# Linear attention with norm and a gated convolution FFN: g_norm as rows, batch 0 by one cast queue, spread products in pairs, a new order, unread products

## Chip, cores and metric

The kernel runs on one core of a Trainium2 chip, in one launch. The metric is the device time in microseconds; the kernel before takes 195.0, the median of three runs (194.63 to 196.04).

## The reference

Eight batches, eight heads, 576 positions, head size 64; the FFN goes from 512 to 1024 and back. All inputs and the output are float32.

```python
kv = np.einsum('bhsd,bhse->bhde', k, v)
out = np.einsum('bhsd,bhde->bhse', q, kv)
rms = np.sqrt(np.mean(out * out, axis=-1, keepdims=True) + 1e-06)
x = out / rms * g_norm            # then (batch, seq, heads * 64) = (8, 576, 512)
h = np.maximum(x @ w_in, 0.0)     # (8, 576, 1024)
conv_out = sum(conv_w[k] * hp[:, k:k + S, :] for k in range(3))   # hp: h padded by one row of zeros on each side
gate = 1.0 / (1.0 + np.exp(-conv_out))
return (h * gate) @ w_out         # (8, 576, 512)
```

## The kernel before

Everything is kept with channels on the partitions and positions on the free axis. The work is cut into small operations with names, and one long string, ORDER, lists them by hand: a loop at the end of the kernel takes the tokens in turn and calls the function of that name. Each engine then runs its own instructions strictly in that order (the last loop of the kernel ties each instruction to the one before it on its engine). A token such as `hm.0.2@2` calls `hm(0, 2)` and gives it buffer slot 2 of its ring. So a buffer's slot, and with it what an operation has to wait for, is written in the order too. There are three PSUM slots of two banks each, ring "a" (heads' transposes, attention output, hidden products, spread products), and two of one bank, ring "b" (kv products, sums of squares, output rows).

For batch b and head pair t (0 to 3) the operations are these.

- `Lq`, `Lk`, `Lv` load one batch of q, k, v from POOL's queue and cast them to bfloat16 on the way (L276). `Li` and `Lo` load halves of w_in and w_out the same way. Batch 0 is loaded in `pre`: head pairs 0 and 1 in float32 by SyncE's queue into a staging tile (L206), cast by `ca` on VectorE (k, v) and ScalarE (q, L305); pairs 2 and 3 by POOL's queue (L217).
- `kv` (L319) makes the 64 by 64 products of k and v of a head; `kvc` copies them into a block diagonal tile, on VectorE for batch 0 and on ScalarE for the others. `qt` transposes q for two head pairs (`qt0` for one, batch 0; L343), and `qc` copies the result on VectorE (`qc0` on ScalarE). `ot` (L373, L374) multiplies the two.
- `sq` squares and `oc` copies that output on ScalarE. `ss` (L427) adds up the squares of all four head pairs into 32 rows each, four products with 32 columns of output. `ln` takes the reciprocal root, and `sl` splits it on VectorE into bfloat16 parts. `sp` (L454) spreads these over the 64 channels of each head: two products per head pair, with all 128 rows of the parts and a selecting matrix, `spread`, of 2048 columns. `mu` (L460) multiplies output, g_norm and root on VectorE. Batch 0 goes another way: `on` spreads and adds in one product, `nl` takes the root, `mu0` multiplies.
- `hm` (L471) is the product with w_in for one block f of 128 hidden channels, eight products of 288 columns; `re` (L479) is the relu on ScalarE. `ta` (L493, L494) multiplies by two of the three taps, `aa` (L500) and `ab` (L506) add, `sg` (L512) is the sigmoid on ScalarE, `mg` (L518) the gating product. A convolution index c stands for one batch or two, by CONV.
- `om` (L528) is the product with w_out for a block m of 128 rows of a pair p of batches, eight products of 512 columns, in two halves for pairs 0 and 3; `ea` (L534) copies it on ScalarE and `st` (L539) stores it by SyncE's queue.
- `ct` and `pc` bring conv_w into channel layout and scale it; `pl`, `ps`, `pn` make the constants sel, spread, na and nb on VectorE. g_norm is loaded straight onto the partitions, as 128 elements of 4 bytes (L209).

The order puts batch 0 through attention first, then batches 1 to 7 in parts between the hidden products.

## Time and profile before

| | us |
|---|---|
| median of three runs (lowest, highest) | 195.0 (194.63, 196.04) |
| span of the profiled execution (the page gives no other time of it) | 192.5 |
| TensorE busy in it | 171.1 (89%) |
| ScalarE busy | 153.5 (80%) |
| VectorE busy | 148.8 (77%) |
| first product of TensorE | 10.31 |
| first product with w_in | 25.90 |
| last product's end, by the chain | 188.75 |

The span runs from the first to the last instruction. The shares are means over the whole span; the stretches differ. A product's record holds its latency, so the start of the next product tells better than the length what one costs. "Granted clock" is what the throttle gave TensorE.

### The profile page before, as it was taken

How to read it: one execution, taken by the hardware profiler on the slowest of the kernel's cores; microseconds unless marked ns; L12 is line 12 of the kernel's file. 1: busy time of each engine (PE TensorE's matmuls, PEld its weight loads, DVE VectorE, ACT ScalarE, POOL GpSimd, SP SyncE). 2: the span in 40 equal slices, each digit the busy share in tenths (PEclk: the TensorE clock that was granted, in tenths of full speed). 3: DMA queues.
4: the chain of work that ended last, by engine and by line, in shares of the span. 5: the costliest groups of instructions: out<-in, count | busy, mean ns of one | idle time of the engine just before them, and what ended most of it. 6: DMA issues, size and time to landing. Idle time of an engine off the chain costs nothing.

```text
span 192.5 us, 4249 instructions
## 1 busy us (share of the span) xinstructions
PE 171.1 (89%) x1753; PEld 106.9 (56%) x1753; DVE 148.8 (77%) x279; ACT 153.5 (80%) x246; POOL 25.7 (13%) x39
## 2 busy tenths in 40 slices
...
DMA  4999999999999997999950000441040010170874
GB/s 135 207 236 204 203 204 203 204 204 206 186 203 204 182 130 118 137 120 188 208 185 5 0 3 0 165 167 54 0 163 3 0 54 3 54 272 0 327 266 170
DMA packets 26517, 26.84 MB, mean 139 GB/s; under 512 B 1388, under 2 KB 21892, under 8 KB 26500
## 3 DMA queue, kind: packets, MB, share of 16 engines
...
q10 hardware_dynamic: 196, 0.01, 0.1%
q14 instruction: 4, 0.03, 0.1%
...
## 4 chain that ended last, share of the span: by engine, by line
PE 70%; DVE 11%; ACT 8%; DMA 6%; issue 2%; SPq 1%; ACTq 0%
PE h_ps L471 28%; PE om_ps L528 27%; DMA stg<-in_q_dram 6%; PE qt_ps L343 4%; PE sp_ps L454 4%; PE kv_ps L319 3%; ACT sq L388 2%; PE o_ps L374 2%; DVE taps L493 2%; DVE taps L500 2%; DVE taps L506 2%; DVE taps L494 1%; ACT o L393 1%; ACT h L479 1%; DVE h L518 1%
## 5 line engine op out<-in xcount | busy, mean ns | idle before, releaser
L471 PE MATMUL h_ps<-xT,w_in_sb 128*128 128x288 bf16 x512 | 70.1, 290 | 0.7 <-ACT o L393 0.3
L528 PE MATMUL om_ps<-w_out_sb,h 128*128 128x512 bf16 x288 | 66.7, 379 | 0.1
L471 PEld LDWEIGHTS <-w_in_sb 128*128 128x128 bf16 x512 | 50.0, 99 | 17.1 <-issue 1.5
L479 ACT ACTIVATE h<-h_ps 128x576 bf16<-128x576 f32 x64 | 40.6, 658 | 9.3 <-PE h_ps L471 9.0
L528 PEld LDWEIGHTS <-h 128*128 128x128 bf16 x288 | 27.8, 98 | 30.2 <-issue 0.7
L512 ACT ACTIVATE taps<-taps,cw 128x576 bf16<-128x576 bf16 (+1 forms) x48 | 42.9, 933 | 1.0 <-DVE taps L506 0.9
L534 ACT ACTIVATE row<-om_ps 128x512 f32<-128x512 f32 x36 | 21.8, 605 | 10.7 <-PE om_ps L528 10.4
L518 DVE TENSOR_TENSOR h<-h,taps 128x1152 bf16<-128x1152 bf16 (+1 forms) x24 | 22.7, 953 | 5.7 <-ACT taps L512 5.7
L500 DVE TENSOR_TENSOR taps<-taps 128x1152 bf16<-128x1152 bf16 (+1 forms) x24 | 23.0, 958 | 0.5
L343 PE MATMUL qt_ps<-ident,q_sb 96*64 96x96 bf16 x384 | 12.6, 221 | 12.0 <-ACT q_sb L305 11.9
L506 DVE TENSOR_TENSOR taps<-taps,h 128x1152 bf16<-128x1152 bf16 (+1 forms) x24 | 22.9, 956 | 0.5
L493 DVE TENSOR_SCALAR taps<-h,cw 128x576 bf16<-128x576 bf16 (+1 forms) x48 | 20.8, 434 | 2.5 <-ACT h L479 2.5
L460 DVE SCALAR_TENSOR_TENSOR xT<-o,g_sb,sp_ps 128x576 bf16<-128x576 f32 x28 | 21.2, 810 | 1.8 <-PE sp_ps L454 1.8
L494 DVE TENSOR_SCALAR taps<-h,cw 128x576 bf16<-128x576 bf16 (+1 forms) x48 | 20.3, 423 | 0.0
L343 PEld LDWEIGHTS <-q_sb 96*64 96x64 bf16 x384 | 10.4, 120 | 15.9 <-ACT q_sb L305 12.4
L388 ACT ACTIVATE sq<-o_ps 128x576 bf16<-128x576 f32 x28 | 18.1, 673 | 0.1
L393 ACT ACTIVATE o<-o_ps 128x576 f32<-128x576 f32 x28 | 17.8, 662 | 0.0
L374 PE MATMUL o_ps<-qT,kvbd 128*128 128x512 bf16 x32 | 12.7, 409 | 0.0
...
L368 DVE COPY qT<-qt_ps 128x1152 bf16<-128x1152 bf16 x14 | 10.4, 754 | 1.7 <-PE qt_ps L343 1.4
L454 PE MATMUL sp_ps<-wparts,spread 128*128 128x288 bf16 x56 | 9.9, 287 | 1.0 <-ACT h L479 0.7
L276 POOL DMA_DIRECT2D q_sb<-in_q_dram x8 | 6.0, 748 | 34.5 <-PE qt_ps L343 29.0
...
## 6 DMA issues: line engine op xcount, KB each, us to landing
...
```

The costliest lines, as they stand in the source:

```text
L343: nc.tensor.transpose(ps[i * D:(i + 1) * D, r * PS:(r + 1) * PS], qkv["q", b][:, 2 * t + i, r * D:(r + 1) * D], ident[:PS, :PS])
L388: nc.scalar.activation(by_r(s), natural(o), AX.Square)
L471: nc.tensor.matmul(ps[:, e, :HS], w_in_sb[:, t, f * P:(f + 1) * P], x[:, t, e * HS:(e + 1) * HS], start=(t == 0), stop=(t == NT - 1))
L479: nc.scalar.activation(T["h", b // 2][:, f, b % 2, :].rearrange("p (e n) -> p e n", e=2), T["hm", b, f][:, :, :HS], AX.Relu)
L493: nc.vector.tensor_scalar_mul(tap[:, 0, f % 2, :n, 8:8 + S], h[:, f], cw[:, f:f + 1])
L494: nc.vector.tensor_scalar_mul(tap[:, 1, f % 2, :n, :S], h[:, f], cw[:, 2 * NF + f:2 * NF + f + 1])
L500: nc.vector.tensor_add(tap[:, 1, :, :n, :S], tap[:, 0, :, :n, 7:7 + S], tap[:, 1, :, :n, 1:1 + S])
L506: nc.vector.tensor_add(y, y, h[:, 2 * j:2 * j + 2])
L512: nc.scalar.activation(y, y, AX.Sigmoid, scale=cw[:, NF + f:NF + f + 1])
L518: nc.vector.tensor_mul(h, h, T["tap", c, j][:, 1, :, :n, :S])
L528: nc.tensor.matmul(T["om", p, m], h[:, f, m * P:(m + 1) * P], w_out_sb[:, f, :], start=(f == 0), stop=(f == NF - 1))
L534: nc.scalar.activation(T["os", p, m], T["om", p, m], AX.Copy)
```

## The change

Six things change.

- g_norm is loaded as a 25th row of the tile that holds conv_w, in two pieces of 64 elements, and comes onto the partitions by the same transpose (`ct`, `pg`). The scaled taps get a tile of their own, cwn.
- Of batch 0 only k and v of head pair 0 go by SyncE's queue and the staging tile. All else goes by POOL's cast queue in the order q0, k1, v1, q1, k2, ..., and the identity's select comes behind the first two of these loads.
- `sp` makes two head pairs at once. Each product takes the 32 rows of the parts that belong to its head pair, at that row of the array (tile_position), and the two head pairs' products alternate. It takes two slots of ring "a". `spread` has 512 columns instead of 2048.
- The tokens may choose the engine: a colon and 1 moves a relu, `oc`, `ea` or `kvc` to VectorE and a q copy to ScalarE. In the new order 7 relus, 9 `oc`, 5 `ea` and 7 `kvc` are on VectorE (the kvc of batch 0 were there before), and 3 of 4 `qc0` and 4 of 14 `qc` on ScalarE. An `oc` on VectorE waits for ScalarE's `sq` of the same output. `pl` moves to POOL.
- `unread` issues n products of 512 columns on a tile of ones, into a PSUM slot that nobody reads: 11, 9, 2, 2, 3 and 6, all ahead of hm.0.0.
- The order is a new one. Batches 4 and 5 are loaded and their kv made before the first product with w_out, and w_out is loaded behind batch 5. `al` allocates the tiles of x and h, whose slots the tokens now give.

```diff
@@ ORDER @@
-pre@0,0,0,1 ca.q.0 qt0.0@0 qc0.0@0 ca.k.0 ca.v.0 kv.0.0.1@0 kvc.0.0.1.0 kvc.0.0.1.1 ot.0.0@1 sq.0.0@0 on.0@2
...
+pre@0,0,0 ca.k.0 ps pi ca.v.0 unread.11@0 kv.0.0.1@0 ct@1 Lv.1.0@1 qt0.0.0@0 Lq.1.0@1 Lk.1.0@1 pg kv.0.1.1@1
+unread.9@1 qt0.0.2@1 Li.0 Lq.1.2 qt0.0.1@2 pc kvc.0.0.1.0@0 qc0.0.0:1@0 kvc.0.1.1.0:1 kvc.0.0.1.1:1 al.x0@0
+qc0.0.2:1@1 al.h1@0 kvc.0.1.1.1 al.h0@1 ot.0.0@0 al.x1@1 sq.0.0@0 unread.2@1 on.0.0@1 nl.0.0@0 kv.0.2.1@0 qc0.0.1:1
+kvc.0.2.1.0 kvc.0.2.1.1 unread.2@1 ot.0.2@1 sq.0.2@1 unread.3@2 on.0.2@2 mu0.0.0 ot.0.1@0 nl.0.2@1 qt0.0.3@2 Lv.1.2
+mu0.0.2 sq.0.1@2 qc0.0.3 Lk.1.2 kv.0.3.1@1 kvc.0.3.1.1 on.0.1@1 nl.0.1@2 qt.1.0@2 kvc.0.3.1.0:1 mu0.0.1 ot.0.3@1
+sq.0.3@3 kv.1.0.2@0 on.0.3@0 qc.1.0@2 nl.0.3@3 mu0.0.3 kvc.1.0.2.0:1@1 Li.1 unread.6@2 hm.0.0@2 hm.0.2@0 kvc.1.0.2.1
+hm.0.3@1 re.0.0:1 pl re.0.2 ot.1.1@2 ta.0.0@0 re.0.3:1 qt.1.1@0 sq.1.1@4 hm.0.1@1 pn Lk.2.0@0 Lv.2.0@0 kv.1.2.2@1
+re.0.1 kvc.1.2.2.0 ot.1.0@1 kvc.1.2.2.1 sq.1.0@5 oc.1.0@4 qc.1.1@3 ta.0.2@1 ta.0.1 oc.1.1:1@5 ot.1.3@0 sq.1.3@6
...
+ta.1.1 oc.3.0@7 qt.4.0@0 re.1.4 sl.1@0 aa.1.0 re.1.2 Lq.5.0@1 sp.3.0@2,1 mu.3.0 mu.3.1 qc.4.0:1@4 Lv.5.0@1 Lk.5.0@1
+sp.2.1@0,2 mu.2.2 mu.2.3 Lo.0 kv.4.0.4@0 Lo.1 sg.0.4 kvc.4.0.4.0@0 kvc.4.0.4.1 sp.2.0@1,0 mu.2.1 mu.2.0 sg.0.5
+ot.4.1@2 sq.4.1@0 qt.5.0@0 oc.4.1@7 ot.4.2@1 sq.4.2@1 mg.0.2 hm.2.2@2 qc.5.0@0 ta.1.2@0 oc.4.2@6 ot.4.3@0 re.2.2
+qt.5.1@1 ab.1.0 sq.4.3@2 oc.4.3@0 hm.1.5@2 qc.5.1@1 sg.1.1 sp.3.1@0,1 kv.5.0.4@1 re.1.5 kvc.5.0.4.0@1 ta.1.3 al.x2@0
+mu.3.3 mu.3.2 hm.2.0@2 kvc.5.0.4.1 sg.1.0 hm.3.2@1 re.2.0 re.3.2 Lv.7.0@0 ot.5.1@0 ot.5.3@2 sq.5.3@3 aa.1.1 mg.1.0
+ab.1.1 om.0.3.0@0 ot.4.0@1 om.0.1.0@1 sg.1.2 sg.1.3 oc.5.3:1@1 Lq.7.0@0 ta.1.4@1 ta.1.5 sq.5.1@4 ot.5.0@2 om.0.3.4
+sq.4.0@5 oc.5.1:1@3 sq.5.0@6 om.0.1.4 hm.3.3@0 ea.0.3:1@0 oc.5.0@2 oc.4.0@4 aa.1.2 mg.1.1 re.3.3 ss.4@0 ot.5.2@2
+sq.5.2@7 hm.3.0@1 ss.5 hm.3.1@0 ln.2@0 re.3.1 ta.1.6@0 Lk.7.0@0 oc.5.2:1@5 ab.1.2 hm.2.4@2 re.3.0 ta.1.7 qt.7.1@0
...
+st.0.0 st.0.1 st.0.5 ta.3.7 sg.2.6 ss.7 mg.2.3 hm.5.4@1 ea.0.7@2 st.0.2 re.5.4 hm.5.0@2 hm.4.0@0 ln.3@0 aa.3.3
+om.1.4.0@0 sl.3@0 ea.1.4@1 ab.3.3 re.5.0 hm.4.1@1 om.1.8.0@1 re.4.1 re.4.0 sp.6.0@2,1 mu.6.1 om.1.5.0@0 sp.7.1@0,1
+st.0.6 ea.1.8@3 om.1.1.0@1 ta.3.0@0 mu.7.3 hm.4.4@1 mu.6.0 mu.7.2 hm.4.3@2 sg.3.6 sg.3.7 hm.5.1@0 mg.3.3 ea.1.1@4
...
+st.1.5 sg.5.1 sg.5.0 ea.3.1@4 aa.5.2 ab.5.2 mg.5.0 st.3.0 re.7.6:1 ta.5.6@0 ta.5.7 sg.5.4 ea.3.3@5 om.2.2.0@0 sg.5.5
+aa.5.3 om.2.5.0@1 st.2.0 ab.5.3 ea.2.2@3 om.3.7.0@0 mg.5.2 ea.2.5@6 st.2.2 sg.5.6 st.3.3 sg.5.7 st.2.6 om.2.1.0@1
+st.2.5 mg.5.3 ea.2.1@7 om.3.7.4 ea.3.7@1 om.3.5.0@1 om.3.8.0@0 om.3.5.4 ea.3.5@3 om.3.8.4 ea.3.8@5 om.3.6.0@1
+om.3.4.0@0 om.3.6.4 st.3.7 st.2.1 st.3.5 om.3.4.4 ea.3.6:1@2 st.3.8 st.3.2 st.3.1 st.3.6 ea.3.4@6 st.3.4
...
+    NC = 3 * NF
+    cw_rows = consts.tile([NC + 1, P], FP32, name="cw_rows")
+    cw = consts.tile([P, NC + 1], FP32, name="cw")
+    g_sb = cw[:, NC:NC + 1]
+    cwn = consts.tile([P, 3, NF], FP32, name="cwn")
+    fill = consts.tile([P, 512], BF16, name="fill")
...
-    spread = consts.tile([P, NT * 4, 2, D], BF16, name="spread")
-    bg = consts.tile([P, NT, 8], BF16, name="bg")
+    spread = consts.tile([P, 4, 2, D], BF16, name="spread")
+    bg = consts.tile([P, 8], BF16, name="bg")
...
@@ -200,74 +205,81 @@
     def pre():
         for x in "qkv":
             qkv[x, 0] = ring(x, [PS, H, R * D], BF16, name=x + "_sb")
-        T["stg"] = ring("h", [PS, 3, 2, 2, R * D], FP32, name="stg")
-        for t in range(2):
-            for x in "kvq":
-                nc.sync.dma_start(out=T["stg"][:, "kvq".index(x), t], in_=heads(x, 0, 2 * t, 2))
-        nc.scalar.dma_start(out=cw_rows, in_=moe_conv_w.rearrange("k (f p) -> (k f) p", p=P))
+        T["stg"] = work.tile([PS, 2, 2, R * D], FP32, name="stg", tag="h0", bufs=1)
+        for i, x in enumerate("kv"):
+            nc.sync.dma_start(out=T["stg"][:, i], in_=heads(x, 0, 0, 2))
+        nc.scalar.dma_start(out=cw_rows[:NC], in_=moe_conv_w.rearrange("k (f p) -> (k f) p", p=P))
         for i in range(2):
-            nc.scalar.dma_start(out=g_sb[i * D:(i + 1) * D, :], in_=g_norm.unsqueeze(1))
+            nc.scalar.dma_start(out=cw_rows[NC:, i * D:(i + 1) * D], in_=g_norm.unsqueeze(0))
+        nc.vector.memset(fill, 1.0)
         nc.vector.memset(ident, 0.0)
-        nc.gpsimd.affine_select(
-            out=ident, in_=ident, compare_op=AL.not_equal, fill=1.0,
-            base=0, pattern=[[-1, P]], channel_multiplier=1)
-        for t in range(2, NT):
-            for x in "kvq":
-                nc.gpsimd.dma_start(out=qkv[x, 0][:, 2 * t:2 * t + 2, :], in_=heads(x, 0, 2 * t, 2))
         nc.vector.memset(kvbd[0], 0.0)
...
-        nc.vector.tensor_copy(ident32, ident[:3 * NF, :3 * NF])
+        for n, (x, t) in enumerate([(x, t) for t in range(NT) for x in "kvq" if t or x == "q"]):
+            if n == 2:
+                nc.gpsimd.affine_select(
+                    out=ident, in_=ident, compare_op=AL.not_equal, fill=1.0,
+                    base=0, pattern=[[-1, P]], channel_multiplier=1)
+            nc.gpsimd.dma_start(out=qkv[x, 0][:, 2 * t:2 * t + 2, :], in_=heads(x, 0, 2 * t, 2))
+
+    @op
+    def pi():
+        nc.vector.tensor_copy(ident32, ident[:NC + 1, :NC + 1])
         for t in taps:
             nc.vector.memset(t[:, 0, :, :, 7:8], 0.0)
             nc.vector.memset(t[:, 1, :, :, S:S + 1], 0.0)
 
     @op
     def ct():
-        T["cw"] = ring("b", [P, 3 * NF], FP32, name="cw_ps", padded_shape=[P, 512])
+        T["cw"] = ring("b", [P, NC + 1], FP32, name="cw_ps", padded_shape=[P, 512])
         nc.tensor.transpose(T["cw"], cw_rows, ident32)
 
     @op
+    def pg():
+        nc.vector.tensor_copy(cw, T["cw"])
+
...
     @op
     def pl():
-        nc.vector.memset(sel, 0.0)
+        nc.gpsimd.memset(sel, 0.0)
         for c in range(4):
             for i in range(2):
                 at = c * 2 + i
-                nc.vector.memset(
+                nc.gpsimd.memset(
                     sel[i * D:(i + 1) * D, c, :].rearrange("p (g c) -> p g c", c=8)[:, :3, at:at + 1], 1.0)
     @op
     def ps():
-        nc.vector.tensor_add(bg, idv[:, :, 0, :], idv[:, :, 1, :])
-        nc.vector.tensor_add(bg, bg, idv[:, :, 2, :])
+        nc.vector.tensor_reduce(
+            bg, ident.rearrange("p (t g c) -> p c t g", t=NT, g=4)[:, :, :, :3],
+            axis=mybir.AxisListType.XY, op=AL.max)
         nc.vector.tensor_copy(
-            spread.rearrange("p a i d -> p (a i) d"),
-            bg.rearrange("p t c -> p (t c)").unsqueeze(2).to_broadcast([P, NT * 8, D]))
+            spread.rearrange("p a i d -> p (a i) d"), bg.unsqueeze(2).to_broadcast([P, 8, D]))
...
     @op
     def ca(x, t):
-        to, fr = qkv[x, 0][:, 2 * t:2 * t + 2, :], T["stg"][:, "kvq".index(x), t]
-        if x == "q":
+        nc.vector.tensor_copy(qkv[x, 0][:, 2 * t:2 * t + 2, :], T["stg"][:, "kv".index(x)])
+
+    def last():
+        return nc.cur_bb.bb.instructions[-1]
+
+    def after(ins, other):
+        if ins.engine != other.engine:
+            tc.add_manual_dep(
+                ins, other.name,
+                mybir.DependencyInfo(mybir.DependencyClass.Sync, mybir.DependencyReason.DATA), reason="bank")
+
+    def copy(to, fr, on_act):
+        if on_act:
             nc.scalar.activation(to, fr, AX.Copy)
         else:
             nc.vector.tensor_copy(to, fr)
@@ -325,11 +348,9 @@
     @op
     def kvc(b, t0, n, i):
         half = slice(i * D, (i + 1) * D)
-        to, fr = kvbd[b % 2][half, t0:t0 + n, half], T["kvps", b, t0][half]
-        if b == 0:
-            nc.vector.tensor_copy(to, fr)
-        else:
-            nc.scalar.activation(to, fr, AX.Copy)
+        if slots:
+            T["kvbd", b] = kvbd[slots.pop(0)]
+        copy(T["kvbd", b][half, t0:t0 + n, half], T["kvps", b, t0][half], pick[0] == 0)
 
...
-    @op
-    def qc0(t):
+    def qt0(b, t):
+        T["qt0", b, t] = ring("a", [P, 1024], BF16, name="qt_ps", padded_shape=[P, 2048])
+        transposes(T["qt0", b, t], b, t)
+
+    @op
+    def qc0(b, t):
         if t % 2 == 0:
-            T["q0", t // 2] = ring("qT", [P, 2, S], BF16, name="qT")
-        T["qT", 0, t] = T["q0", t // 2][:, t % 2, :]
-        nc.scalar.activation(by_r(T["qT", 0, t]), natural(T["qt0", t][:, :S]), AX.Copy)
+            T["q0", b, t // 2] = ring("qT", [P, 2, S], BF16, name="qT")
+        T["qT", b, t] = T["q0", b, t // 2][:, t % 2, :]
+        copy(by_r(T["qT", b, t]), natural(T["qt0", b, t][:, :S]), pick[0] == 1)
...
-        nc.vector.tensor_copy(s, T["qtps", b, u][:, :, :S])
+        copy(s, T["qtps", b, u][:, :, :S], pick[0] == 1)
+
+    @op
+    def unread(n):
+        nfill[0] = n
+        fills(ring("a", [P, 1024], FP32, name="unread_ps"))
+
+    def fills(ps):
+        for _ in range(nfill[0]):
+            nc.tensor.matmul(ps[:, :512], fill[:, :P], fill, start=True, stop=True)
...
     @op
     def ot(b, t):
         ps = T["ot", b, t] = ring("a", [P, 1024], FP32, name="o_ps")
-        mm576(ps, kvbd[b % 2][:, t, :], T["qT", b, t])
+        fills(ps)
+        mm576(ps, T["kvbd", b][:, t, :], T["qT", b, t])
...
+        T["sqi", b, t] = last()
 
     @op
     def oc(b, t):
         s = T["o32", b, t] = ring("o32", [P, S], FP32, name="o32")
-        nc.scalar.activation(by_r(s), natural(T["ot", b, t][:, :S]), AX.Copy)
-
+        copy(by_r(s), natural(T["ot", b, t][:, :S]), pick[0] == 0)
+        after(last(), T["sqi", b, t])
+
+    @op
+    def on(b, t):
+        ps = T["on", b, t] = ring("a", [P, 1024], FP32, name="on_ps")
+        fills(ps)
+        mm576(ps, ones, T["sq", b, t])
+
...
+    @op
+    def al(what):
+        p = int(what[1:])
+        if what[0] == "x":
+            T["x", p] = ring("xT", [P, NT, 2, S], BF16, name="xT")
+        else:
+            T["h", p] = ring("h", [P, NF, 2, S], BF16, name="h")
 
     def x_tile(b):
-        if ("x", b // 2) not in T:
-            T["x", b // 2] = ring("xT", [P, NT, 2, S], BF16, name="xT")
         return T["x", b // 2][:, :, b % 2, :]
...
     @op
-    def sp(b, t):
+    def sp(b, u):
         g = NG[b]
         bi = NORM[g].index(b)
-        ps = T["sp", b, t] = ring("a", [P, 2, 512], FP32, name="sp_ps")
+        for t in (2 * u, 2 * u + 1):
+            T["sp", b, t] = ring("a", [P, 2, 512], FP32, name="sp_ps")
         for e in range(2):
-            nc.tensor.matmul(
-                ps[:, e, :HS], spread[:, t * 4 + 2 * bi + e, :, :].rearrange("p i d -> p (i d)"), T["w", g],
-                start=True, stop=True)
+            for t in (2 * u, 2 * u + 1):
+                rows = slice(t * 32, (t + 1) * 32)
+                nc.tensor.matmul(
+                    T["sp", b, t][:, e, :HS], spread[rows, 2 * bi + e, :, :].rearrange("p i d -> p (i d)"),
+                    T["w", g][rows], start=True, stop=True, tile_position=(t * 32, 0))
...
     @op
     def hm(b, f):
         ps = T["hm", b, f] = ring("a", [P, 2, 512], FP32, name="h_ps")
         x = x_tile(b)
+        fills(ps.rearrange("p e n -> p (e n)"))
...
     @op
     def re(b, f):
-        if b % 2 == 0 and f == 0:
-            T["h", b // 2] = ring("h", [P, NF, 2, S], BF16, name="h")
-        nc.scalar.activation(
-            T["h", b // 2][:, f, b % 2, :].rearrange("p (e n) -> p e n", e=2),
-            T["hm", b, f][:, :, :HS], AX.Relu)
+        to = T["h", b // 2][:, f, b % 2, :].rearrange("p (e n) -> p e n", e=2)
+        fr = T["hm", b, f][:, :, :HS]
+        if pick[0] == 0:
+            nc.scalar.activation(to, fr, AX.Relu)
+        else:
+            nc.vector.tensor_scalar(to, fr, 0.0, None, op0=AL.max)
...
-        nc.vector.tensor_scalar_mul(tap[:, 0, f % 2, :n, 8:8 + S], h[:, f], cw[:, f:f + 1])
-        nc.vector.tensor_scalar_mul(tap[:, 1, f % 2, :n, :S], h[:, f], cw[:, 2 * NF + f:2 * NF + f + 1])
+        nc.vector.tensor_scalar_mul(tap[:, 0, f % 2, :n, 8:8 + S], h[:, f], cwn[:, 0, f:f + 1])
+        nc.vector.tensor_scalar_mul(tap[:, 1, f % 2, :n, :S], h[:, f], cwn[:, 2, f:f + 1])
...
-        nc.scalar.activation(T["os", p, m], T["om", p, m], AX.Copy)
+        copy(T["os", p, m], T["om", p, m], pick[0] == 0)
...
     for token in ORDER.split():
         what, _, at = token.partition("@")
+        what, _, n = what.partition("+")
+        what, _, choice = what.partition(":")
         slots[:] = [int(s) for s in at.split(",")] if at else []
+        pick[0], nfill[0] = int(choice or 0), int(n or 0)
```

## The prediction

> **What bounds the kernel now.** I read the table of stretches first. Its columns are the length, then the busy us and count of PE, PEld, DVE, ACT and POOL, the granted clock, the DMA share and GB/s.
>
> ```profile
> 30.00:36.00 6.00, 5.45 (x77) 3.42 (x72) 5.86 (x16) 5.72 (x13) 3.80 (x5) 1.00 1.32 204
> 36.00:48.00 12.00, 10.84 (x160) 7.61 (x160) 10.04 (x19) 11.74 (x21) 0.07 (x1) 1.00 1.30 204
> 48.00:60.00 12.00, 11.45 (x187) 7.34 (x186) 11.08 (x24) 11.84 (x23) 3.79 (x5) 1.00 1.27 197
> 60.00:172.00 112.00, 111.51 (x1064) 71.59 (x1063) 103.77 (x163) 102.55 (x160) 5.61 (x7) 1.00 0.46 98
> ```
>
> From 60 us on TensorE has no gaps, so it is the bound there. Before 60 it has some, ScalarE is full, and the loads run flat out at 204 GB/s. The DMA line of the page says how long they do:
>
> ```profile
> DMA  4999999999999997999950000441040010170874
> GB/s 135 207 236 204 203 204 203 204 204 206 186 203 204 182 130 118 137 120 188 208 185 5 0 3 0 165 167 54 0 163 3 0 54 3 54 272 0 327 266 170
> ```
>
> So I split the time in two: until about 60 us, where several things press, and after it, where only TensorE's products count. Then the start, in TensorE's timeline (start, length, line; a run's length contains the latency of its last product):
>
> ```profile
> 22.88 0.61 PE L374 MATMUL o_ps<-qT,kvbd 128*128 128x512 bf16 x1
> 25.90 3.52 PE L471 MATMUL h_ps<-xT,w_in_sb 128*128 128x288 bf16 x16
> 29.28 0.38 PE L374 MATMUL o_ps<-qT,kvbd 128*128 128x512 bf16 x1
> ```
>
> A 512-column product takes 0.61 at 22.88 and 0.38 at 29.28. TensorE works at half speed until about 28.5, though the granted clock reads 1.00 throughout. Last, what the first loads cost (queue, packets, MB, share), in the stretch 4.0 to 7.5:
>
> ```profile
> q0 software_dynamic: 235, 0.17, 36.4%
> q1 hardware_dynamic: 226, 0.31, 29.5%
> q10 hardware_dynamic: 150, 0.00, 2.2%
> ```
>
> 461 data packets in 3.5 us are 132 per us; around 13 us the cast queue alone moves 131 in half a us. The slow stretch has 150 packets of q10 in it, nearly all 4-byte elements of g_norm, and it ends when they end.
>
> **TensorE after 60 us.** I price products by start to start, from chain rows: eight of L471 in 0.98 (0.1225 each), 72 of L528 in 15.55 (0.216), 48 of L319 in 0.88 (0.0183), 24 transposes in 0.63; a product of 576 columns is 0.24. At 59.86 the kernel before begins om.0.3.0. By its order 272 products of om, 50 hm, 24 sp, 4 kv, 16 ot, 7 qt and 4 ss are left: 126.4 us. The last ends at 188.75, 128.9 later. So losses after 60 us are only 2.5.
>
> In the new order I take kv.5.0.4 as the mark, because its k is the last load in front of the first w_out. From it on, 288 products of om, 47 hm, 8 paired sp, 3 kv, 13 ot, 4 qt and 4 ss are left. With two products of a pair at a time (0.25 per op) that is **119.5 us**. That two run at once is not shown for rows, but ss shows it for columns:
>
> ```profile
> 91.80 0.65 PE L471 MATMUL h_ps<-xT,w_in_sb 128*128 128x288 bf16 x4
> 92.39 0.67 PE L427 MATMUL ss_ps<-sq,sel 128*32 128x288 bf16 x16
> 92.99 1.04 PE L528 MATMUL om_ps<-w_out_sb,h 128*128 128x512 bf16 x4
> ```
>
> Sixteen products of 128*32 take 0.60 until the next starts; at four at a time they are 4 x 0.1225 = 0.49. Of the rest, 0.11 is spent leaving; entering, 91.80 + 0.49 to 92.39, costs 0.10. So a pair op costs 0.25 + 0.2 where the four products before cost 0.49. Bounds: 0.25 (no gaps) to 0.70 (gaps and no overlap). I take 0.45, the row of ss being the nearest. Eight ops then lose 1.6. The Trainium skill, TensorEngine Tiling (Array Packing), section Tiling Modes, speaks against the pairs: a change of tiling mode drains TensorE. The gaps of 0.10 and 0.11 agree; without such drains the sum would be 1.6 lower.
>
> Losses after the mark: 2.5 as before plus 1.6, rounded to **4.0** (2.4 to 6.0).
>
> **When kv.5.0.4 starts: the loads.** One q, k or v of a batch lands as 0.59 MB; at 204 GB/s it takes 2.9 us. Before, q of batch 2 lands at 22.66 + 15.3 = 38.0. Until then 6.36 MB had to pass (three batches and w_in), 31.2 us: start and lag are 6.8. The change sends 2 transfers by SyncE and 10 by POOL's one queue in place of 6 and 6, which alters no byte to land. It replaces 128 elements of g_norm by two rows. If that frees 4.0 to 7.5, 456 packets, or 1.7 us, are won: 5.1 remain. Bounds: 4.5, as POOL's first load goes out ahead of the identity, one us earlier; 6.8, if the slow stretch has another cause. I take 5.1, since the slow stretch ends with those elements. POOL now issues v, q, k of batch 5 ahead of Lo.0 and Lo.1. Six batches and w_in are 11.67 MB, 57.2 us: k of batch 5 lands at **62.3** (61.7 to 64.0). Behind it Lo.0 lands at 64.9, just as om.0.3.0 (3.3 us of products later) wants it. POOL waits for freed buffers, but stays some transfers ahead.
>
> **When kv.5.0.4 starts: VectorE.** The first 11 unread products run from about 1.1 (the fill memset at 0.8, 0.27 by the kvbd row) to 5.8, while the cast of v ends no earlier (5.06 + 0.71): free. The transpose ct now stands ahead of the first q in TensorE's queue and waits for the rows of g_norm; even at 2.0 + 6.7 = 8.7, when the second half of its elements landed, it costs some 1.5 us at the start. POOL's select comes behind two loads (0.75 + 0.64), at 2.2 for 1.0; its first reader, ps, follows the cast of k at 4.6. The 9 stand in front of q of head pair 2, landing at about 11: free if warm (1.9), 1 us late if cold (3.8). The 2, 2 and 3 lie behind a Square of 0.65, the 6 behind a rsqrt of 0.74 and a mu0 of 0.82. Cover gone, all of them cost 0.43 each, but TensorE has 9 us spare, see below. From ot.0.0 at 11.4 ScalarE needs 4 x 0.65, 4 x 0.74, a q copy and three kv copies, 6.9 in all; with TensorE's turns in between and the last mu0, hm.0.0 starts at about 22 (21.3 to 23) instead of 25.9, and warm.
>
> From there to kv.5.0.4 TensorE has 31.3 us of products: ready at 53.3, so it idles some 9 us. VectorE has 10 mu, 7 q copies, 11 ta, 5 aa, 5 ab, 4 mg, 2 sl, 3 relu, 6 oc. Spacing by rows:
>
> ```profile
> 97.67 5.16 DVE L460 SCALAR_TENSOR_TENSOR xT<-o,g_sb,sp_ps 128x576 bf16<-128x576 f32 x7 [0.52 <-PE sp_ps L454]
> ```
>
> 0.74 a mu; 0.28 a tap, 0.67 an aa, ab or mg, 1.75 an sl, 0.68 a q copy from the same timeline. Relu and oc on VectorE have no row: between ScalarE's 0.54 and mu's 0.74 I take 0.68. Sum 37.3 from 23.1: 60.4 without a gap, 62.4 at 95%. So loads and VectorE meet at the mark. The whole kernel moves 7 relus, 9 oc, 5 ea and some kv copies to VectorE and 7 q copies back, about +10 us there and -8 on ScalarE; after the mark VectorE has 105 us for the 112 until om.3.7.4 needs its last mg, so it is covered by 7 us at the end, and least at om.1.4.0: mg.2.3 comes 49.3 us of VectorE's work after the mark, om.1.4.0 50.3 of TensorE's. If VectorE loses more than 1 us there, TensorE pays the rest; the 6.0 above holds that. An oc on VectorE also waits for ScalarE's Square (0.65); taps are queued behind it, and it is in the 95%. The smaller constants (spread a quarter as long, sel on POOL, pc shorter, two casts fewer) take some 3 us off VectorE ahead of 22 and are not on the path. The stores of pair 0 move behind the loads in SyncE's queue, where nothing waits but eight row slots.
>
> **Sum.** 62.3 + 119.5 + 4.0 = 185.8 for the last product. Behind it, as before, a copy and a store:
>
> ```profile
> 173.20 15.55 PE om_ps L528 x72
> 188.78 0.60 ACT row L534
> ```
>
> 192.5 - 188.75 = 3.75. Span 189.55 against 192.5. The page gives only the span; the median of the runs, 195.0, is 2.5 above it, so **192.0**.
>
> **Rivals.**
> *Tighter.* No drains at pairs, loads at 61.7, VectorE at 98% as in 30 to 36: 61.7 + 119.5 + 2.4 + 3.75 + 2.5 = 189.9, and below 189 if the lag of a load is shorter too. For it: such a VectorE share exists. Against it: the gaps around ss. Chance 0.18.
> *Slow first loads stay.* The stretch from 4.0 is not g_norm's: 64.0, so 193.7. For it: the cast queue is just starting up there. Against: SyncE's queue is slow too. Chance 0.12.
> *VectorE sets the first 60 us, slower than before.* Place: the waits of mu, oc and q copies behind three PSUM slots, of which each pair op takes two. If VectorE keeps only the share that it had in 36 to 48, 10.04 of 12, then 37.3 becomes 44.6: 23.1 + 44.6 = 67.7, and 197.4. It decides from 65.3 (a share of 0.88), where the gain is gone. For it: in 30 to 60 the share was 0.90, with 10 us less moved there. Against: ScalarE was the full one then. Chance 0.20. A clock that stays low until 22 would push the same way, by about 1 to 2.
>
> **How the numbers follow.** The forecast has 0.50, with its own range 189.7 to 194.3. A measurement here tells about 1% from no change (193.05 and 196.95). Of the 0.50, 0.36 are faster, 0.13 the same, 0.01 slower; of *tighter* all 0.18 faster; of *slow loads* 0.03, 0.08 and 0.01; of *VectorE* 0.06 the same and 0.14 slower. Sum: 0.57, 0.27, 0.16. The range, 188.0 to 197.4, reaches into both outer cases.
>
> **What would show it.** Right: 512-column products at 0.38 well before 20; L471 first at 21 to 23; no slow DMA stretch at 4 to 7.5; gaps of 0.5 to 2 us on TensorE for loads between 30 and 62; kv.5.0.4 near 62; 0.45 per pair op; hardly a gap after. Wrong: TensorE waiting for VectorE or ScalarE after 70 us, pair products start to start at 0.12 each, or kv.5.0.4 away from 62 by more than 3.

## Result and the profile after

The changed kernel takes **196.45 us**, the median of 20 runs (195.30 to 201.53). The kernel before, run beside it, takes 194.63 (20 runs, 193.74 to 196.04). The ratio is 1.0083, with a 95% interval of 1.0063 to 1.0104: slower by 0.8%, where 192.0 was predicted. Here and below, the medians are of all executions, while the ratios leave out those more than 1.5% above the fastest of their kernel, most of which have an unusually low granted clock; where the two differ, the ratio is the better measure.

The profiled execution of the changed kernel took 196.67, with a span of 194.9. First the table of stretches. Its columns are the length, then the busy us and count of PE, PEld, DVE, ACT and POOL, the granted clock, the DMA share and GB/s.

```profile
30.00:36.00 6.00, 3.88 (x36) 2.56 (x37) 5.89 (x12) 5.78 (x10) 1.31 (x2) 1.00 1.32 203
36.00:48.00 12.00, 11.10 (x214) 7.74 (x215) 11.20 (x21) 10.87 (x19) 3.19 (x4) 1.00 1.27 193
48.00:60.00 12.00, 9.71 (x200) 6.33 (x196) 11.30 (x21) 11.67 (x19) 3.03 (x4) 0.97 1.31 204
60.00:72.00 12.00, 11.71 (x149) 7.32 (x146) 9.69 (x16) 10.01 (x18) 4.64 (x6) 0.75 1.28 205
72.00:172.00 100.00, 100.00 (x839) 60.10 (x838) 94.55 (x150) 84.72 (x125) 0.00 (x0) 1.00 0.33 85
```

From 72 us on TensorE has no gap at all. Ahead of that it has more than before: 3.88 of 6 busy from 30 to 36 (5.45 before) and 9.71 of 12 from 48 to 60 (11.45 before), while VectorE and ScalarE are both nearly full. And a thing is new: from 60 to 72 the granted clock averages 0.75. The page's rows of clock and GB/s:

```profile
PEclk9999999999995799999999999999999999999999
...
GB/s 150 181 191 205 203 204 204 203 194 187 204 204 204 206 207 201 203 80 3 161 57 2 108 0 3 3 214 0 3 0 89 126 132 194 108 103 9 214 254 177
```

The clock is at half from 59.3 to 66.1 us. The loads start cleanly (the 135 of the first slice was 150 here) and run flat out to 84 us. TensorE's timeline shows the warm start, the pairs and the cold stretch (start, length):

```profile
12.05 0.38 PE L404 MATMUL o_ps<-qT,kvbd 128*128 128x512 bf16 x1
...
62.97 2.13 PE L515 MATMUL h_ps<-xT,w_in_sb 128*128 128x288 bf16 x8
...
66.40 1.15 PE L515 MATMUL h_ps<-xT,w_in_sb 128*128 128x288 bf16 x8
67.49 0.42 PE L497 MATMUL sp_ps<-wparts,spread 32*128 32x288 bf16 x4
67.83 0.95 PE L342 MATMUL kv_ps<-v_sb,k_sb 96*64 96x64 bf16 x48
```

A 512-column product takes 0.38 at 12.05, where the kernel before was still at 0.61 at 22.88. Eight hidden products take 2.13 at 62.97 and 1.15 at 66.40. The mark of the prediction, kv.5.0.4, is the last row: 67.83. From the start of a pair operation to the start of what follows it are 67.83 - 67.49 = 0.34 to 0.35. But the eight hidden products ahead of it take 67.49 - 66.40 = 1.09, where eight cost 0.98 by the prediction's rows; this is taken up below. The end of the chain:

```profile
170.85 19.96 PE om_ps L573 x92
...
190.88 0.60 ACT row L328
```

### The profile page after: what moved, and what is told of

It is laid out like the page before. It is cut to its first block, busy times and chain, and to the rows that moved or that the text cites. A ratio compares the mean times of both kernels' runs of the same rounds, so it can differ in the third digit from the quotient of the medians.

```text
span 194.9 us, 4305 instructions
## 1 busy us (share of the span) xinstructions
PE 178.1 (91%) x1786; PEld 104.9 (54%) x1786; DVE 157.2 (81%) x282; ACT 146.6 (75%) x227; POOL 28.9 (15%) x52
## 4 chain that ended last, share of the span: by engine, by line
PE 75%; ACT 9%; DVE 7%; DMA 3%; POOL 2%; issue 2%; POOLq 0%; ACTq 0%
PE om_ps L573 32%; PE h_ps L515 29%; PE qt_ps L364 4%; DMA q_sb<-in_q_dram 3%; PE o_ps L404 3%; PE kv_ps L342 2%; PE sp_ps L497 2%; ACT h L524 1%; ACT kvbd L328 1%; ACT qT L328 1%; DVE xT L503 1%; ACT sq L419 1%; DVE o L330 1%; ACT sq L417 1%; DVE taps L545 1%
## 5 line engine op out<-in xcount | busy, mean ns | idle before, releaser
L557 ACT ACTIVATE taps<-taps,cwn 128x576 bf16<-128x576 bf16 (+1 forms) x48 | 42.9, 936 | 2.2 <-DVE taps L551 2.0
L524 ACT ACTIVATE h<-h_ps 128x576 bf16<-128x576 f32 x57 | 35.5, 654 | 8.7 <-PE h_ps L515 7.2
L328 ACT ACTIVATE row<-om_ps 128x512 f32<-128x512 f32 x31 | 18.2, 597 | 15.9 <-PE om_ps L573 14.2
L503 DVE SCALAR_TENSOR_TENSOR xT<-o,cw,sp_ps 128x576 bf16<-128x576 f32 x28 | 21.5, 809 | 1.6 <-PE sp_ps L497 1.6
L539 DVE TENSOR_SCALAR taps<-h,cwn 128x576 bf16<-128x576 bf16 (+1 forms) x48 | 20.5, 426 | 0.0
L538 DVE TENSOR_SCALAR taps<-h,cwn 128x576 bf16<-128x576 bf16 (+1 forms) x48 | 19.9, 415 | 0.2
L364 PE MATMUL qt_ps<-ident,q_sb 96*64 96x96 bf16 x384 | 12.0, 215 | 2.7 <-DMA q_sb<-in_q_dram 1.6
L328 ACT ACTIVATE o<-o_ps 128x576 f32<-128x576 f32 x19 | 12.5, 667 | 0.0
L400 PE MATMUL unread_ps<-fill 128*128 128x512 bf16 x33 | 9.7, 436 | 2.1 <-DVE fill L215 1.5
L453 DVE SCALAR_TENSOR_TENSOR xT<-o_ps,cw,o 128x576 bf16<-128x576 f32 x4 | 3.3, 817 | 10.2 <-ACT o L438 10.2
L330 DVE COPY qT<-qt_ps 128x1152 bf16<-128x1152 bf16 (+1 forms) x11 | 8.3, 750 | 2.1 <-PE qt_ps L364 2.1
```

The costliest lines, as they stand in the source:

```text
L328: nc.scalar.activation(to, fr, AX.Copy)
L364: nc.tensor.transpose(ps[i * D:(i + 1) * D, r * PS:(r + 1) * PS], qkv["q", b][:, 2 * t + i, r * D:(r + 1) * D], ident[:PS, :PS])
L503: nc.vector.scalar_tensor_tensor(x_tile(b)[:, t, :].rearrange("p (e n) -> p e n", e=2), T["o32", b, t].rearrange("p (e n) -> p e n", e=2), ...
L524: nc.scalar.activation(to, fr, AX.Relu)
L538: nc.vector.tensor_scalar_mul(tap[:, 0, f % 2, :n, 8:8 + S], h[:, f], cwn[:, 0, f:f + 1])
L539: nc.vector.tensor_scalar_mul(tap[:, 1, f % 2, :n, :S], h[:, f], cwn[:, 2, f:f + 1])
```

## Experiments

Two groups of names: kernels on the changed kernel, and kernels called e_old, which have the changed kernel's front up to hm.0.0 and behind it the order of the kernel before; e_before_g_rows is the kernel before with one edit. All ratios are to the kernel before. The last two columns are each from one profiled execution. hm.0.0 differs there by up to 1.1 us between kernels with the same front, so the distance from hm.0.0 to kv.5.0.4 tells more than either alone.

| kernel | us, median | ratio, 95% interval | hm.0.0 | kv.5.0.4 |
|---|---|---|---|---|
| changed kernel | 196.45 | 1.0083, 1.0063 to 1.0104 | 23.12 | 67.83 |
| e_before_g_rows | 193.33 | 0.9909, 0.9873 to 0.9946 | 24.60 | |
| e_old_order | 190.82 | 0.9789, 0.9755 to 0.9823 | 22.54 | 61.22 (other order) |
| e_old_no_unread | 194.43 | 0.9960, 0.9925 to 0.9994 | 24.40 | |
| e_old_pairs_adjacent | 190.38 | 0.9770, 0.9734 to 0.9807 | 22.53 | |
| e_unpaired | 195.88 | 1.0045, 1.0020 to 1.0069 | 22.87 | 66.24 |
| e_warm | 195.25 | 1.0033, 1.0002 to 1.0064 | 22.06 | 65.63 |
| e_light_vector | 195.83 | 1.0038, 1.0002 to 1.0073 | 22.32 | 66.79 |
| e_light_scalar | 195.87 | 1.0049, 1.0022 to 1.0075 | 22.88 | 66.06 |
| e_light_both | 194.42 | 0.9966, 0.9935 to 0.9997 | 22.73 | 64.84 |
| e_light_warm | 194.26 | 0.9987, 0.9962 to 1.0012 | 22.36 | 64.27 |
| e_w_out_early | 198.13 | 1.0172, 1.0135 to 1.0209 | 22.97 | 69.43 |
| e_engines_back | 206.88 | 1.0535, 1.0476 to 1.0593 | 22.85 | 73.56 |

### Which part costs: the order

The theory was that the start and the pairs gain and that the new order behind hm.0.0 loses more.

**e_old_order**: the token string is the changed kernel's up to hm.0.0, then that of the kernel before.

```diff
-sq.0.3@3 kv.1.0.2@0 ... unread.6@2 hm.0.0@2 hm.0.2@0 kvc.1.0.2.1 ...
+sq.0.3@3 kv.1.0.2@0 ... unread.6@2 hm.0.0@0 re.0.0 pl kvc.1.0.2.1 hm.0.1@2 ot.1.0@1 ...
-    sp(b, u): two head pairs, 32 rows each
+    s1(b, t): one head pair, 128 rows
```

> The changed kernel's front up to hm.0.0 (g_norm as rows, one cast queue for batch 0, 33 unread products), and from hm.0.0 on the order, the load order and the engines of the kernel before, with its spread products over all 128 rows, unpaired. Theory (the new order behind hm.0.0 is what costs: it makes VectorE and ScalarE set TensorE's pace up to 58 us and its gaps let the granted clock fall): the kernel before took 166.6 us from hm.0.0 (25.90) to its end (192.5), so hm.0.0 at 23.1 gives a span of 189.7 and 192.2 us, ratio 0.987, with no stretch of low granted clock. Rival, loads: what follows hm.0.0 in the kernel before waits for its loads, which do not come earlier, so the 2.8 us at the start are given back and the time stays 194.6. Rival, the new start itself costs (33 unread products, two copies instead of six, g_norm through TensorE): 195.5 or more.

It took 190.82, 1.4 below the expectation and 5.6 below the changed kernel. hm.0.0 starts at 22.54 and the last product ends at 185.05: 162.5 later, against 162.8 in the kernel before. So the start's gain is kept to the end, and the loads don't take it back. Its table of stretches:

```profile
36.00:48.00 12.00, 11.30 (x177) 8.11 (x172) 10.57 (x20) 11.76 (x22) 2.32 (x3) 1.00 1.30 205
48.00:60.00 12.00, 11.46 (x139) 6.65 (x139) 10.21 (x22) 11.30 (x20) 1.53 (x2) 1.00 1.31 204
60.00:72.00 12.00, 12.00 (x154) 8.98 (x153) 11.53 (x22) 11.75 (x20) 2.09 (x3) 1.00 1.21 195
```

ScalarE is as full as in the changed kernel, VectorE a little less, but TensorE gets 11.46 of 12 from 48 to 60 and the clock stays at 1.00. So it is what stands behind hm.0.0 that costs. This run takes back the order, the loads, the engine choices and the pairs together; the runs below on the pairs (e_unpaired), the engine choices (e_engines_back) and the loads (e_w_out_early) show that none of these three carries the loss, which leaves the order.

**e_old_no_unread**: e_old_order with the six unread tokens taken out.

```diff
-... ca.v.0 unread.11@0 kv.0.0.1@0 ... kv.0.1.1@1 unread.9@1 qt0.0.2@1 ... nl.0.3@3 mu0.0.3 kvc.1.0.2.0:1@1 Li.1 unread.6@2 hm.0.0@0
+... ca.v.0 kv.0.0.1@0 ... kv.0.1.1@1 qt0.0.2@1 ... nl.0.3@3 mu0.0.3 kvc.1.0.2.0:1@1 Li.1 hm.0.0@0
```

> e_old_order without the 33 unread products, which prices them alone. Theory (they keep TensorE's clock up from 4.7 to 7 us on, and most of them fill waits): the first products run at half rate until 13 to 29 us, hm.0.0 at 24 to 25 instead of 22.5, and 1.5 to 2.5 us more, 192.3 to 193.3. Rival (the clock is granted early without them, or the chain through ScalarE and VectorE hides it): 190.8 or less, by up to the 2.3 us that the last six of them (1.38 us) and others stand ahead of hm.0.0.

194.43, so the 33 products are worth 3.6 us by the medians and 3.3 by the ratios, more than the 1.5 to 2.5 expected. Two rows of TensorE's timeline, first without them, then with:

```profile
17.93 0.61 PE L404 MATMUL o_ps<-qT,kvbd 128*128 128x512 bf16 x1
...
24.40 3.77 PE L525 MATMUL h_ps<-xT,w_in_sb 128*128 128x288 bf16 x16 [0.83 <-ACT o L439]
```

```profile
11.68 0.38 PE L405 MATMUL o_ps<-qT,kvbd 128*128 128x512 bf16 x1
...
22.54 1.63 PE L526 MATMUL h_ps<-xT,w_in_sb 128*128 128x288 bf16 x12
```

Without them TensorE runs at half speed until about 28 (the clock record starts its 1.00 at 27.8; with them at 6.3). hm.0.0 is 1.9 later, and its first products are slow too. The unread products do not keep the clock up in every execution: e_old_order_pairs and e_old_pairs_nine (below) have the same front, and in their profiled executions the clock falls to half at 12.91 and 13.38 us, for 13.65 us each time, and hm.0.0 comes at 25.55 and 25.96.

**e_before_g_rows**: the kernel before with only this part of the change; the transpose ct and the copies out of it move up, ahead of nl.0.

```diff
-            nc.scalar.dma_start(out=g_sb[i * D:(i + 1) * D, :], in_=g_norm.unsqueeze(1))
+            nc.scalar.dma_start(out=cw_rows[NC:, i * D:(i + 1) * D], in_=g_norm.unsqueeze(0))
...
+        nc.vector.tensor_copy(g_sb, T["cw"][:, NC:])
```

> The kernel before, with g_norm loaded as a 25th row of cw_rows and transposed with it, and the copies out of that transpose right behind it, ahead of nl.0. It does that part of the change alone. Theory of the prediction (the 128 elements of 4 bytes make the slow stretch of the other loads from 4 to 7.5 us, 461 packets in 3.5 us): the q load that the chain waits for lands about 1.7 us earlier, the first transposes start at 8.5 instead of 10.3, and all of it follows: 193.2 us, ratio 0.991. Rival (the slow stretch is that of the first loads whatever g_norm does): first transposes at 10.3, 194.9.

193.33 where 193.2 was expected. The stretch from 4 to 7.5 us, first of the kernel before, then of this one:

```profile
4.00:7.50 3.50, 0.00 (x0) 0.00 (x0) 1.27 (x2) 0.00 (x0) 2.73 (x5) 1.00 0.68 139
```

```profile
4.00:7.50 3.50, 0.00 (x0) 0.00 (x0) 1.15 (x2) 0.00 (x0) 2.71 (x5) 1.00 1.03 219
```

139 GB/s became 219 when two rows of 64 elements took the place of 128 elements of 4 bytes each; no other load was changed. The whole front is worth 194.88 - 190.82 = 4.1, less than the sum of these two parts, so they overlap, or its other edits cost; these weren't run by themselves.

### The pairs

**e_unpaired**: the changed kernel, each pair operation as four products over 128 rows.

```diff
-                    T["sp", b, t][:, e, :HS], spread[rows, 2 * bi + e, :, :].rearrange("p i d -> p (i d)"),
-                    T["w", g][rows], start=True, stop=True, tile_position=(t * 32, 0))
+                    T["sp", b, t][:, e, :HS], spread[:, t * 4 + 2 * bi + e, :, :].rearrange("p i d -> p (i d)"),
+                    T["w", g], start=True, stop=True)
```

> The changed kernel with its spread products over all 128 rows, in the same places, four in sequence instead of two pairs. Theory (pairs gain 0.14 us each, but those ahead of the mark are hidden behind VectorE's pace): eight pairs behind the mark, 1.1 us more, 197.6 us. If all fourteen count: 2.0 us more, 198.4. Rival (the pairs are what makes the changed kernel slower, by holding up the products around them): at or below 195.5.

195.88, so the pairs gain nothing in the changed kernel. The theory priced a pair at 0.35 against 0.49, and that leaves out what the pair costs the products ahead of it. The same place of the order in both timelines, first with the pair, then without:

```profile
103.67 1.03 PE L573 MATMUL om_ps<-w_out_sb,h 128*128 128x512 bf16 x4
104.63 0.42 PE L497 MATMUL sp_ps<-wparts,spread 32*128 32x288 bf16 x4
104.98 1.04 PE L573 MATMUL om_ps<-w_out_sb,h 128*128 128x512 bf16 x4
```

```profile
102.39 1.03 PE L573 MATMUL om_ps<-w_out_sb,h 128*128 128x512 bf16 x4
103.25 0.65 PE L497 MATMUL sp_ps<-wparts,spread 128*128 128x288 bf16 x4
103.74 1.03 PE L573 MATMUL om_ps<-w_out_sb,h 128*128 128x512 bf16 x4
```

The pair takes 0.35 and the four unpaired products 0.49, but the four output products ahead take 0.96 with the pair and 0.86 without. So a pair costs 0.35 + 0.10 = 0.45 in all and gains 0.04 here. In front of kv products an unpaired operation costs 0.58 (35.67 to 36.25), and there a pair gains 0.14. From kv.5.0.4 to the last product e_unpaired takes 123.4 (66.24 to 189.68), 0.5 more than the changed kernel.

Ahead of the mark there is nothing to gain on TensorE, which waits there, and in the profile of e_unpaired the clock doesn't fall, where it is at half for 6.8 us in the changed kernel. Its mean is 0.995 or more in ten of twelve executions of e_unpaired, and 0.991 or less in all twenty of the changed kernel. So the pairs' gain of 0.5 behind the mark stands against a lower clock ahead of it. That the pairs bring the clock down because TensorE has less to do fits this; no run tests it alone.

In the order of before, pairs were made at three places: **e_old_order_pairs** (eleven pairs, some moved past other work), **e_old_pairs_adjacent** (four that stood side by side) and **e_old_pairs_nine**.

```diff
-sp: s1.1.1@2 s1.1.0@1
+sp: s2.1.1.1.0@2,1
```

> As e_old_order, and 22 of the 28 spread operations joined into 11 pairs of 32 rows each, the other six with 32 rows but alone. Theory (pairs gain: 0.35 us start to start for four products in the changed kernel's trace, against 0.49 in the kernel before): 11 x 0.14 = 1.5 us below e_old_order, 190.7 us if that one is at 192.2. Rival, pairs cost (the change of tile size holds up the products around them, or a pair takes two buffers at once and makes others wait): not below e_old_order. The prediction's size (0.45 an operation): 0.4 us below it.

> e_old_order with eight of its 28 spread operations, those that stand next to each other, joined into four pairs, and nothing else changed (the other twenty stay over 128 rows). Theory (a pair takes 0.35 us for 0.49, and what made e_old_order_pairs slower than e_old_order was that its other pairs take two buffers at once and move work past each other): 0.3 to 0.6 us below e_old_order, 190.3. Rival (a pair holds up the products around it): 191.2 or more.

> e_old_order with nine pairs instead of e_old_pairs_adjacent's four: all places where two spread operations follow each other on TensorE, the first one's product on VectorE moved behind the pair where it stood between them; the other ten stay over 128 rows. Theory (0.14 us a pair, wherever TensorE has no wait): 9 x 0.14 = 1.3 us below e_old_order where four gave 0.44, so 189.6 to 190.0. Rival (a pair that waits for both buffers gives its gain back, as e_old_order_pairs did): 190.5 to 191.5.

Ratios: 0.9856 (0.9814 to 0.9898) for eleven, 0.9770 for four, 0.9799 (0.9759 to 0.9840) for nine, against 0.9789 for none. Four may gain 0.4 us, which can't be told from nothing; nine gain no more, and eleven take 192.11, 1.3 us more than none. e_old_pairs_adjacent is the fastest kernel of the study, level with e_old_order. The expected 0.14 us a pair is not found in the time, as the 0.04 above would have it.

### The clock

**e_warm**: nine more unread products in the waits from 47 to 58 us, in buffers of ring b.

```diff
-sp.3.0@2,1 ... sp.2.1@0,2 ... kv.4.0.4@0 ... ot.4.1@2
+ub.3@1 sp.3.0@2,1 ... ub.2@1 sp.2.1@0,2 ... ub.2@1 kv.4.0.4@0 ... ub.2@1 ot.4.1@2
```

> The changed kernel with nine more unread 512-column products, in one-bank buffers, at four places between 47 and 58 us where TensorE waits (ahead of sp.3.0, sp.2.1, kv.4.0.4 and ot.4.1). Clock theory (the fall of the granted clock to 0.50 from 59 to 66 us costs 3 us of its own): no stretch under 0.9, kv.5.0.4 at about 65, 193.5 us, ratio to before 0.994. Rival (VectorE sets the pace up to 68 us whatever TensorE's clock is, so a warm clock only moves the waits): 196 us or more, kv.5.0.4 still near 68. If the clock falls all the same, in spite of the nine: 196.5 to 197.

In the profiled execution the clock stays at 1.00 and kv.5.0.4 comes 43.6 behind hm.0.0 instead of 44.7. The median, 195.25, is 1.2 below the changed kernel, not 3. In five of the twelve executions the clock still fell (means of 0.949 to 0.991); the other seven have a median of 195.05. So the low clock is worth 1.0 us (by the ratios) to 1.4: TensorE was slow at a time when it would mostly have waited for others.

### Why the mark is late

The rival of the prediction, VectorE, gave the mark within 0.2 us. These runs take its work away.

**e_light_vector** and **e_light_scalar**: the tokens aa.0 and ab.0, or sg.0, are taken out. **e_light_both**: all of them. **e_light_warm**: e_light_both with e_warm's products.

```diff
-aa.0.0 aa.0.1 ab.0.0 ab.0.1 aa.0.3 ab.0.3 aa.0.2 ab.0.2
-sg.0.1 sg.0.3 sg.0.2 sg.0.0 sg.0.7 sg.0.6 sg.0.4 sg.0.5
```

> The changed kernel without the two additions of each of the four tap pairs of batch 0's convolution (aa.0 and ab.0, eight VectorE instructions of 0.755 us, 6.0 us, all between hm.0.0 and kv.5.0.4). It shows what VectorE's work is worth there. Theory (VectorE sets the pace between 24 and 58 us): kv.5.0.4 starts at 63 to 64.5 instead of 67.8, held from there by k of batch 5, which landed at 63.4; 192.5 to 193.5 us. Rival, ScalarE (11.67 of 12 us busy from 48 to 60) sets it: kv.5.0.4 within 1 us of 66 to 68 and 195.5 or more. Rival, loads set it: the same.

> The changed kernel without the sigmoids of batch 0's convolution (sg.0: eight ScalarE instructions of 0.77 us, 6.2 us, and the one or two table loads of 1.28 us between them, all ahead of kv.5.0.4). Theory, after e_light_vector moved kv.5.0.4 by nothing and e_engines_back by 6 us the wrong way: ScalarE sets the pace ahead of the mark. Then hm.0.0 to kv.5.0.4 takes 40 to 42 us instead of 44.7 (loads of batch 5 hold it from there), and the time is 192.5 to 194. Rival: both engines stand in the chain in turn, so that 8 us off one of them alone gives 1 us or less: 195 or more. Rival, loads: no change.

> The changed kernel without both: batch 0's eight tap additions on VectorE (6.0 us) and its eight sigmoids and their table loads on ScalarE (6.2 us and 1.3 to 2.6). Theory (the two engines are both nearly full between 24 and 58 us and take turns in the chain, so each alone hides the other's relief): hm.0.0 to kv.5.0.4 takes 39.5 to 41.5 us instead of 44.7, held from there by k of batch 5 (63.4), and the time is 192 to 193.5, well below the 195.8 of either alone. Rival, loads: 195.5, kv.5.0.4 still 43 us or more behind hm.0.0. Rival, TensorE's own clock and waits between its own steps: the same.

> e_light_both (no additions, sigmoids and their table loads of batch 0's convolution) with e_warm's nine unread products between 47 and 58 us. Theory (the changed kernel's mark at 67.8 is 62.3 to 63.4 of loads, 3 to 4 us that VectorE and ScalarE add between them, and 1 to 2 us of low clock): kv.5.0.4 at 63.4 to 64.3, that is 40.7 to 41.8 behind hm.0.0, no stretch of low clock, and 191.8 to 193 us. Rival (the engines relieved, nothing is left for the clock; the nine products only take time): 194.4 or more and kv.5.0.4 at 65 or later.

From hm.0.0 to kv.5.0.4 it is 44.7 us in the changed kernel, 44.5 with less VectorE work, 43.2 with less ScalarE work, 42.1 with less of both. Both expectations of a clear gain by one engine failed, and both engines together gave less than expected (39.5 to 41.5, and 192 to 193.5 us). The stretches from 48 to 60 say why one alone doesn't help, first the light VectorE (busy DVE is the third number, ACT the fourth), then the light ScalarE:

```profile
48.00:54.00 6.00, 4.73 (x66) 2.90 (x65) 4.63 (x9) 5.88 (x10) 3.01 (x4) 1.00 1.31 202
54.00:60.00 6.00, 4.55 (x92) 2.75 (x89) 5.45 (x10) 5.61 (x10) 0.00 (x0) 0.82 1.32 204
```

```profile
48.00:54.00 6.00, 4.95 (x92) 3.14 (x87) 6.00 (x12) 4.63 (x10) 3.04 (x4) 1.00 1.32 204
54.00:60.00 6.00, 4.64 (x97) 3.01 (x96) 5.89 (x12) 3.56 (x6) 0.32 (x1) 1.00 1.31 205
```

Each time the other one is nearly full. The changed kernel's chain passes from engine to engine there:

```profile
51.51 0.66 ACT o L328
...
53.38 1.28 ACT L201
...
56.45 0.52 DVE wparts L486
...
57.56 0.82 DVE xT L503
...
58.42 0.40 PE sp_ps L497 x3
```

But with both relieved, and the clock held up (e_light_warm), the stretch is still 41.9 us, where 40.7 to 41.8 was expected, and the time 194.26, where 191.8 to 193 was. k of batch 5 lands at 62.1 there, 2.1 ahead of its use, so the loads don't hold it either. A part of the miss has a reason: without sg.0 the sigmoid's table is loaded later, in front of sg.1, and kv.5.0.4 to om.0.3.0 takes 4.65 instead of 3.54. So 14 us of work off the two engines bring 1.7 against e_warm. They are a part of the cause, and not the whole.

**e_engines_back**: the suffix ":1" is taken from re, oc, ea, kvc and qc behind hm.0.0.

```diff
-re.0.0:1 ... oc.1.1:1@5 ... qc.2.1:1@4 ... ea.0.3:1@0
+re.0.0 ... oc.1.1@5 ... qc.2.1@4 ... ea.0.3@0
```

> The changed kernel with the 28 copies and relus behind hm.0.0 that it gives to the other engine put back on the engine of the kernel before (ahead of kv.5.0.4: six copies of o and three relus back to ScalarE, two copies of qT back to VectorE; 5.2 us less on VectorE, 4.5 more on ScalarE). Theory of the order (both engines together are too full ahead of the mark, and ScalarE has 0.3 us in 12 to spare from 48 to 60): no gain, 196 to 199. Rival (the moves to VectorE are what makes the changed kernel slow): 193 to 195.

206.88, by the ratios 9 more than the changed kernel, worse than the theory's 196 to 199. In the profiled execution (207.47) kv.5.0.4 starts at 73.56, and the clock is at half from 61.78 for 10.24 us. From 54 to 60 ScalarE is at 5.97 of 6 and VectorE at 2.55:

```profile
54.00:60.00 6.00, 4.35 (x74) 3.20 (x73) 2.55 (x8) 5.97 (x11) 0.00 (x0) 1.00 1.31 204
```

The new order needs its engine choices; they are not the fault.

**e_w_out_early**: the loads Lo.0 and Lo.1 stand ahead of Lk.4 and not behind Lk.5.

```diff
-hm.1.0@2 Lk.4.0@0 ... mu.2.3 Lo.0 kv.4.0.4@0 Lo.1 sg.0.4
+hm.1.0@2 Lo.0 Lo.1 Lk.4.0@0 ... mu.2.3 kv.4.0.4@0 sg.0.4
```

> The changed kernel with the two loads of moe_w_out issued ahead of k of batch 4 instead of behind k of batch 5, nothing else. All loads of batches 4 and 5 behind them come about 5 us later: k of batch 5 at 68.4 instead of 63.4. If the engines set the pace up to the mark (67.8), the loads have 4.4 us of slack at kv.5.0.4 and less at qt.5: 196.5 to 198.5. If the loads set it: 5 us more, 201. It also prices that part of e_outputs_early, which took 205.2.

198.13, as the theory of the engines has it. k of batch 5 now lands at 49.6 + 19.8 = 69.4, and at last TensorE waits for it:

```profile
69.43 0.95 PE L342 MATMUL kv_ps<-v_sb,k_sb 96*64 96x64 bf16 x48 [0.65 <-DMA k_sb<-in_k_dram]
```

Six us more of load delay cost 1.6: in the changed kernel, k landed at 63.4, 4.4 ahead of its use.

### Moves that made it worse

Four tries to move a few steps cost 7 to 16 us each, by the ratios.

**e_outputs_early** moves w_out's loads, sg.0.4, sg.0.5, mg.0.2 and three output blocks ahead of the mark; **e_old_outputs_late** moves four output blocks of e_old_order back; **e_o_first** and **e_old_o_first** let the copy of o go before its square, so that a buffer is given back sooner. One line of each kind:

```diff
-qc.4.0:1@4 Lv.5.0@1 ... sp.3.0@2,1 mu.3.0
+qc.4.0:1@4 ... om.0.3.0@0 om.0.3.4 sp.3.0@2,1 mu.3.0
```

```diff
-om.0.1.0@0 sg.0.7 ... hm.3.7@0 kvc.4.0.4.0@0
+sg.0.7 ... om.0.1.0@0 om.0.1.4 hm.3.7@0 kvc.4.0.4.0@0
```

```diff
-            nc.scalar.activation(by_r(s), natural(o), AX.Square)
+            nc.scalar.activation(s, T["o32", b, t], AX.Square)
```

> The changed kernel with the two loads of moe_w_out moved from behind k of batch 5 to behind q of batch 4, sg.0.4, sg.0.5 and mg.0.2 moved up behind mg.0.3, and three output blocks (om.0.3, om.0.1, om.0.0, 5.3 us of products, with their evictions) moved from behind kv.5.0.4 to ahead of sp.3.0, sp.2.1 and ot.4.1, where TensorE waits. Theory (the new order puts work that VectorE and ScalarE must do ahead of 58 us and every output product behind it, so TensorE waits before and is full after): the blocks fill waits as e_warm's nine unread products did, and are then missing behind, so 3 to 4 us below e_warm's 195.25: 191.7, with no stretch of low clock. Rival, loads (w_out ahead of k, v of batch 4 and all of batch 5 makes those 5 us later and TensorE waits for them instead): 195 to 197. Rival, VectorE and ScalarE are so full that three evictions more push everything: 195.

> e_old_order with its first four output blocks (om.0.1, om.0.2, om.0.3, om.0.0, 7.0 us of products, and their evictions) moved from ahead of kv.5.0.4 to behind kv.4.0.4, one each ahead of hm.3.7, hm.2.3, hm.3.3 and hm.2.2, where TensorE was full. Theory (output products, which need one ScalarE copy of 0.6 us for 1.76 us of TensorE, are what fills TensorE while ScalarE and VectorE pace the rest; the new order has none of them before 71 us): hm.1.1 comes only 2 to 4 us earlier than 58.3 though 7 us of products ahead of it are gone, and the time rises by 3 to 5 us over e_old_order, 194 to 196, perhaps with a stretch of low clock. Rival: it is not the output blocks, and the time stays within 1 us of 190.8.

> The changed kernel with the two readers of each o product (batches 1 to 7) in the other order: the copy of o out of its buffer comes first, at the place of the square, and the square is then taken from the copy, at the place of the copy (or just ahead of ss). The same instructions on the same engines; the buffer is given back after the copy and not after both. Theory (turnover of the three two-bank buffers paces TensorE up to kv.5.0.4): the 15 o products there hold a buffer for 1.9 us instead of 2.5, 9 buffer-us or 3 us of the stretch less: hm.0.0 to kv.5.0.4 in 41.5 to 42.5 instead of 44.7, and 193 to 194 us. Rival (the work of VectorE and ScalarE sets the pace): 44 or more and 196 to 197. Rival (the square now comes later, and the norm chain that waits for it, ss to wparts, loses what the buffers gain): 195.5 to 197.5 with TensorE's longest wait at sp.1.0 and sp.3.0.

> e_old_pairs_adjacent with the same swap of o's two readers (there both on ScalarE; o's buffers are held 3.05 us each). Theory of the buffers: TensorE waits less where o products stand close, but behind 60 us it hardly waits at all, so 0.5 to 2 us below 190.4: 188.4 to 189.9. Rival (the later square delays the norm chain): 190.4 to 192.

They took 205.18, 207.38, 206.36 and 200.15 (ratios 1.0425, 1.0614, 1.0462 and 1.0271), above every theory and every rival that stood for them. In e_outputs_early w_out has landed at 54.6, but om.0.3.0 starts at 59.78: the moved sigmoids and the gating product behind them stand in front of a copy of o on VectorE, the hidden products wait for the buffer that this copy frees, and the output block stands behind them. e_old_outputs_late bears out half of its theory: with 7.0 us of products gone ahead of it, hm.1.1 comes only 2.3 earlier (56.05 for 58.30), TensorE is busy 2.91 of 6 us from 48 to 54, and the clock falls at 54.4 for 6.8 us. But the rest of its 16 us is of another kind, since the moved blocks share one buffer, which ScalarE frees late. The view of the waits, from 48 to 100 us (total, times, longest):

```profile
PE om_ps L584 <- ACT row L329: 6.8, 4, 2.3
```

e_o_first does shorten the hold of o's buffers, from 2.5 to 1.6 us each on average, and kv.5.0.4 still comes 50.0 behind hm.0.0. (A hold is taken from the first product's start to the last reader's end.) The hidden products' buffers are held longer instead, 2.5 for 2.2, and the sums of squares wait for the later squares, by its view of the waits from 24 to 80 us:

```profile
PE ss_ps L464 <- ACT sq L418: 3.5, 2, 2.1
```

Its profiled execution (207.47) also has the clock at half for 10.24 of the 13.65 us from 58.99 on, which is part of the 50.0. So buffers as the pace are not borne out; as the swap brings a delay of its own, they are not ruled out either. These four runs say little of the cause that they were made for, and much of the order: each queue is served in order, so a step that comes late holds up everything behind it.

## Why the prediction was wrong, step by step

The sum was 62.3 + 119.5 + 4.0 + 3.75 + 2.5. In the profiled execution of 196.67 it came out as 67.83 + 119.5 + 3.5 + 4.1 + 1.8: the last product ends at 190.80, the span at 194.9. **The step that failed is the first term**, kv.5.0.4 at 62.3; it was 5.5 late, and the other terms come out 0.9 below theirs. The prediction let the landing of k set this start, with VectorE ready at the same time and TensorE 9 us early. k landed at 63.4, 1.1 late, and kv.5.0.4 started 4.4 behind that: VectorE, ScalarE and TensorE were not ready for it.

- *Start.* hm.0.0 at 23.12, predicted 22 (21.3 to 23). The row of g_norm did what was foreseen: the loads started clean, and k of batch 5 landed at 63.4, within its bounds (61.7 to 64.0). That the unread products keep the clock up was right and undervalued: the sum gave them no price, and in e_old_order they are worth 3.3 to 3.6.
- *VectorE up to the mark.* "62.4 at 95%" failed. Its work there was 39.7 us busy, not 37.3, and that was a share of 0.89 of the 44.7. Worse, ScalarE was never added up for this stretch. It has 38.1 us in the same 44.7. By the prediction's prices the new order has 31.3 us of products there, so 2.5 us of engine work for each us of products. e_old_order has from hm.0.0 to its own kv.5.0.4 31.9 and 35.8 us on the two engines for 33.2 of products: 2.0. It has four whole output blocks in that stretch, which keep TensorE busy 6.9 us for four copies of 0.6. The new order has none until w_out has landed at 66 and 68.5. That is the difference seen in the traces; the runs that moved blocks didn't settle how much of the loss it is.
- *The clock.* It had no place in the sum behind the start. It fell because TensorE was idle too often (nine unread products in the waits kept it up), and cost 1.0 to 1.4 (e_warm).
- *What stays open.* Of the 13.4 us that the stretch takes beyond its products, the clock has 1.1, and 14 us less work on the two engines take off 1.7, by e_light_warm against e_warm. e_old_order loses 5.5 in its stretch too (38.7 for 33.2). Some 5.1 of the new order's loss have no cause that a run has shown. By the trace TensorE idles 6.0 us in the stretch (2.8 in that of e_old_order), in twelve kinds of short waits, the longest 1.5 and none for a load; the other 7.4 are products that take longer than their price, in the cold stretch or alone behind a wait.
- *Behind the mark.* Right: 123.0 for 119.5 + 4.0. A pair operation costs the 0.45 that was foreseen, and for the reason given: about 0.25 for products two at a time, 0.10 on leaving, and 0.10 more in the products ahead of it. The Trainium skill, TensorEngine Tiling (Array Packing), section Tiling Modes, says that a change of mode drains TensorE; the 0.10 on either side agrees with it. Against the 0.49 of four unpaired products this leaves next to no gain.
- *The rivals.* "VectorE sets the first 60 us" gave 67.7 and 197.4, nearly the measured mark. Its price was right and its mechanism only half: 6 us less on VectorE moved kv.5.0.4 against hm.0.0 by 0.2. A mark that agrees isn't yet a cause. Its condition should have been written for both engines.
- *What would show it.* Of the list, the 0.38 products, the end of the slow stretch, the 0.45 per pair and the full TensorE afterwards came true; the waits for loads between 30 and 62 didn't. Of the signs of being wrong, kv.5.0.4 more than 3 from 62 came true.
